# A fused retention layer and two MLPs: four mixed steps issued as 24 products, two outputs, two scores

## The chip, the cores and the metric

The kernel runs on one core of a Trainium2 chip. The core has five engines with a queue of instructions each: TensorE (PE) multiplies matrices, VectorE (DVE), ScalarE (ACT) and GpSimd (POOL) work on elements, SyncE (SP) starts the DMA transfers here. An engine takes its instructions in the order in which the program issues them; engines wait for each other by semaphores. The metric is the time of one execution on the device in microseconds (us); lower is better.

## The reference

A retention layer (linear attention with a decay per head) gives x, and two MLPs follow it. In float32, cut to the core:

```python
for t in range(S):                                   # B=2, H=8, S=768, D=64
    state = gamma * state + outer(k[t], v[t])
    y[t] = (1 / sqrt(D)) * q[t] @ state
x = y as (1536 tokens, 512)
h = x @ w_in;  g = softplus(h);            x = g @ w_out      # 512 -> 2048 -> 512
h = x @ w_in2; g = s * relu(h) ** 2 + b;   return g @ w_out2
```

## The kernel before

**Retention.** The 768 positions of a batch are cut into 6 chunks of 128; with 2 batches there are 12 chunks, and each is worked on in two units of four heads, so there are 24 units. A unit has *scores* (`att_scores`, L150: 8 small matmuls k by q into PSUM, then the decay mask on DVE writes tile `a`) and *outputs* (`att_out`, L173: `st` by `q2`, `a` by v, and the update of the state into the right half of the same PSUM bank). What follows a unit's outputs is in `unit` (L430): ACT copies the output to `xh` (`x_hi`), DVE adds the update to the decayed state (`sm`), ACT writes it to `st` in two pieces and decays the state of the unit before (`sg`, two pieces), and DVE writes the rest `xl` (`x_lo`). POOL scales q and v of the next chunk.

**MLPs.** A float32 operand is split into a high part (`xh`, `wh`, `gh`) and a low part (`xl`, `wl`, `gl`), and a product of two is three matmuls: 12 for a step's h (`h_mm`) and 12 for its share of the output sums (`acc_mm`). A step is a block of 128 hidden units by a tile of 512 tokens. `act_0` to `act_3` make g from h, `act_hi` (ACT) and `act_lo` (POOL or DVE) split it. `acc_mm` of a step is issued three steps later in the first part of the program, and two later after that. Four steps make a group; then `take_out` (L370) copies the four sums out of PSUM.

**Weights.** A float64 weight half comes by DMA and is put together and split by `split_w` (L259): three DVE instructions write the word `wx` (before step 3 a lent PSUM bank, `acc`), ACT squares (`wm<-raw`), a fourth DVE instruction writes `wm`, ACT copies it to `wh`, POOL subtracts to get `wl`. `fill(n)` issues the next n of these four DVE stages; the last stage brings `wh` and `wl` with it.

**Order.** It is written out by hand (`manual_schedule`). First eight units run alone (L506). Steps 0 to 2 (`early`, L519) have h products and two units each, with two units' score banks in turn: `un`, and two lent accumulation banks, whose mask is two DVE instructions (L168). Steps 3 to 7 (`mixed`, L536) have in turn: 12 h products, a unit's outputs, scores of a later unit, 12 sum products, the second unit's outputs, scores. The step's weight half is finished (`fill(2)`) at its very end, after both units and both masks. The half that `mixed` or its successor finishes in step 3, 4 or 5 is the one that `acc_mm` of the next step uses: halves (1,1), (2,1) and (3,1), the second number 1 being the half for the sums. In step 6 the sums of steps 0 to 3 are copied out on ACT, and step 7 begins new sums in their banks. From step 8 on (L567) there are only products: 40 steps of 24.

Of the kernel before, what the change touches and what calls it, by code (L numbers as in the profile page):

```python
# [7 lines left out]
F32 = mybir.dt.float32  # L8
# [3 lines left out]
ALU = mybir.AluOpType  # L12

P = 128
# [4 lines left out]
C = 128  # L19
# [26 lines left out]
def tile_retention_mlps(ctx: ExitStack, tc: tile.TileContext, qk, kv, w1, w2, sb, consts, out):  # L46
# [8 lines left out]
    wp = ctx.enter_context(tc.tile_pool(name="w", bufs=RING))  # L55
    gp = ctx.enter_context(tc.tile_pool(name="g", bufs=LAG_U + 1))
    tp = ctx.enter_context(tc.tile_pool(name="t", bufs=2))
    ps_acc = ctx.enter_context(tc.tile_pool(name="ps_acc", bufs=4, space=bass.MemoryType.PSUM))
    ps_h = ctx.enter_context(tc.tile_pool(name="ps_h", bufs=1, space=bass.MemoryType.PSUM))
    ps_y = ctx.enter_context(tc.tile_pool(name="ps_y", bufs=1, space=bass.MemoryType.PSUM))  # L60
    ps_s = ctx.enter_context(tc.tile_pool(name="ps_s", bufs=1, space=bass.MemoryType.PSUM))

    def bank(pool, tag):
        return pool.tile([P, 512], F32, tag=tag, name=tag)

    cst = cp.tile([P, CW], F32, tag="cst", name="cst")
    vtab = cst[:, 0:H]
# [18 lines left out]
        return scored[0] == NU and not a_t  # L86


    ac = [bank(ps_acc, "acc") for _ in range(KC)]

    def word():
        if fill.at >= LAG_U:
# [46 lines left out]
    def scale_q(ci):  # L139
# [7 lines left out]
        )  # L147
        q2_t[ci] = t

    def att_scores(n, banks):  # L150

        ci, f = divmod(n, HF)
        t = qk_t[ci]

        def of(h):
            return banks[h] if isinstance(banks, tuple) else banks[:, h, :HC]

        for i in range(HP):
            p = f * HP + i
            for h in range(2):  # L160
                r = slice(h * D, (h + 1) * D)
                nc.tensor.matmul(  # L162
                    of(h)[:, i * C : (i + 1) * C], t[r, 1, p], t[r, 0, p], start=True, stop=True
                )
        a = ap_.tile([P, 2, HC], F32, tag="a", name="a")
        if isinstance(banks, tuple):
            for h in range(2):
                nc.vector.tensor_tensor(out=a[:, h], in0=banks[h], in1=mask[:, f, h], op=ALU.mult)  # L168
        else:
            nc.vector.tensor_tensor(out=a, in0=banks[:, :, :HC], in1=mask[:, f], op=ALU.mult)  # L170
        a_t[n] = a

    def att_out(n, y):  # L173
# [119 lines left out]
    steps = [(la, g, j, f4) for la in range(2) for g in range(NG) for j in range(NTILE) for f4 in range(FG)]  # L293
    h_t, l_t, gg_t, acc_t = {}, {}, {}, {}

    def h_mm(s, part):
        la, g, j, f4 = steps[s]
        wh, wl = w_t[la * NF + g * FG + f4, 0]
        if part == 0:
            h_t[s] = bank(ps_h, "h") if s < SB or s % 2 else bank(ps_y, "y")  # L300
        ps = h_t[s]
        for cc in (0, 1) if part == 0 else (2, 3):
            wa, wb = (w[:, cc * P : (cc + 1) * P] for w in (wh, wl))
            for i, (l, r) in enumerate(((wa, xh), (wa, xl), (wb, xh))):
                nc.tensor.matmul(  # L305
                    ps, l, r[j][:, cc, :], start=cc == 0 and i == 0, stop=cc == KC - 1 and i == 2
                )
# [14 lines left out]
    def act_1(s):  # L322
        if steps[s][0] == 0:

            nc.scalar.activation(l_t[s], l_t[s], AF.Softplus)  # L325
# [24 lines left out]
    def act_lo(s, eng=None):  # L350
        gh, gl = gg_t[s]
        (eng or nc.vector).tensor_tensor(out=gl, in0=l_t.pop(s), in1=gh.bitcast(F32), op=ALU.subtract)  # L352

    def acc_mm(s, banks):
        la, g, j, f4 = steps[s]
        wh, wl = w_t[la * NF + g * FG + f4, 1]
        gh, gl = gg_t[s]
        if (la, g, j) not in acc_t:
            acc_t[la, g, j] = [bank(ps_acc, "acc") for _ in range(KC)] if acc_t else ac
        for cc in banks:  # L360
            cs = slice(cc * P, (cc + 1) * P)
            ps = acc_t[la, g, j][cc]
            if la == 0:
                ops = ((wh[:, cs], gh), (wh[:, cs], gl), (wl[:, cs], gh))
            else:
                ops = ((gh[:, cs], wh), (gh[:, cs], wl), (gl[:, cs], wh))
            for i, (l, r) in enumerate(ops):
                nc.tensor.matmul(ps, l, r, start=f4 == 0 and i == 0, stop=f4 == FG - 1 and i == 2)  # L368
# [76 lines left out]
                load_next()  # L445
            load_kv(ci + NIN)

    def score_to(n, banks):
        while scored[0] < min(n, NU):
            att_scores(scored[0], banks(scored[0]))  # L450
            scored[0] += 1

    def own(n):
        return un

    def lent(n):

        return un if n % HF == 0 else (ac[0][:, :HC], ac[1][:, :HC])

    def out_of(y):  # L460
        return y[:, :HC], y[:, HC : HC + HP * D]
# [15 lines left out]
    with tc.manual_schedule():  # L477
        fill.at = -1
        nc.scalar.preload_act_table_set("softplus")
        nc.vector.memset(zero, 0.0)  # L480
        nc.vector.memset(st, 0.0)
        nc.vector.memset(cu[:, 0:1], 0xC0000000)
        nc.vector.memset(cu[:, 1:2], 29)
        load_qk(0)
        nc.sync.dma_start(out=cst[:, :CG], in_=consts[:, :CG])
        load_kv(0)
        nc.sync.dma_start(out=cst[:, CG:], in_=consts[:, CG:])
        load_qk(1)
        load_kv(1)
        load_qk(2)  # L490
        load_next()
        load_kv(2)
        load_qk(3)
        load_kv(3)

        def warm(bank, key):
            for _ in range(WARM[key]):
                nc.tensor.matmul(bank[:, 0:P], zero[:, 0:P], zero[:, P : 2 * P], start=True, stop=True)

        ys = [bank(ps_h, "h"), bank(ps_y, "y")]  # L500
        warm(ac[3], "first")
        scale_q(0)
        scale_v(0)
        score_to(2, lent)
        warm(ac[3], "u0")
        for n in range(N0):  # L506
            if n >= len(ys):
                ys.append(bank(*((ps_h, "h"), (ps_y, "y"))[n % 2]))
            unit(n, out_of(ys[n]))
            if n == 1:  # L510
                load_next()
                load_next()
                nc.sync.dma_start(out=sbt, in_=sb)
                warm(ac[3], "s2")

            score_to((2, 4, 4, 6, 7, 8, 9, 10)[n], lent)
            fill((0, 0, 0, 2, 1, 1, 0, 4)[n])

        def early(s):  # L519

            fill.at = s
            n = N0 + HF * s
            h_mm(s, 0)
            h_mm(s, 1)
            act_0(s)
            unit(n, out_of(bank(ps_y, "y")), lambda: act_1(s))
            score_to(n + 3, lent)
            act_2(s)
            act_3(s)
            unit(n + 1, out_of(ac[3]))  # L530
            act_hi(s)
            score_to(n + 4, lent)
            act_lo(s, nc.gpsimd)
            fill(4)

        def mixed(s):  # L536

            old = s - LAG_U
            fill.at = s
            n = N0 + HF * s  # L540
            h_mm(s, 0)
            h_mm(s, 1)
            act_0(s)
            unit(n, out_of(bank(ps_y, "y")), lambda: act_1(s))
            score_to(n + 3, own)
            act_2(s)
            act_3(s)
            act_hi(s)
            fill(2)
            acc_mm(old, FIRST)  # L550
            acc_mm(old, SECOND)
            unit(n + 1, out_of(bank(ps_y, "y")))
            score_to(n + 4, own)
            act_lo(s, nc.gpsimd)
            if steps[old][3] == FG - 1:
                for cc in range(KC):
                    take_out(old, cc)
            fill(2)

        for s in range(SB):  # L560
            (early if s < LAG_U else mixed)(s)
        for old in range(SB - LAG_U, SB - LAG):
            acc_mm(old, FIRST)
            acc_mm(old, SECOND)
        fill(left[0])
        work = iter(())
        for s in range(SB, NS + LAG):  # L567
            run, old, prev = s < NS, s - LAG, s <= NS
            takes = steps[old][3] == FG - 1
            late = work  # L570
            work = split_next(s + 1) if run and not takes else iter(())
            if run:
                h_mm(s, 0)
                h_mm(s, 1)
                act_0(s)
            if prev and s > SB:
                act_3(s - 1)
            go(work, 2)
            if run:
                acc_mm(old, FIRST)  # L580
                if takes:
                    take_out(old, 0)
                    take_out(old, 1)
                act_1(s)
            if prev and s > SB:
                act_hi(s - 1)
            if run:
                act_2(s)
            go(late, 1)
            if prev and s > SB:  # L590
                act_lo(s - 1)
            if run:
                acc_mm(old, SECOND)
                if takes:
                    take_out(old, 2)
                    take_out(old, 3)
            go(work, 2)

        for banks in (FIRST, SECOND[:1], SECOND[1:]):
            for old in (NS - 2, NS - 1):  # L600
                acc_mm(old, banks)
            for cc in banks:
                take_out(NS - 1, cc)
# [70 lines left out]
```

## Time and profile before

| | |
|---|---|
| time, median of 3 runs | 587.14 us (587.09 to 587.19) |
| profiled execution | 587.26 us, span 585.3 us |
| busy, share of the span | PE 98%, DVE 78%, ACT 38%, POOL 23% |
| PE clock granted | 9 tenths or more in all 40 slices |
| chain that ended last | PE 91%, DVE 4%, ACT 2% |

The span is the time from the first instruction to the last; 1.96 us of the profiled execution lie outside it. A busy engine counts from the start to the modelled end of its instructions, and matmuls overlap by about 0.16 us, so PE's own pace is read from the starts of its instructions. A row of a timeline has the start, the length, the engine, the line and operation, the tiles written and read, the shape, the count of merged instructions, and in brackets the idle time before it with what ended it.

### The profile page before, as it was taken

To read this page: it belongs to the slowest core of one execution; us is meant where nothing else is said; L and a number is where in the kernel's file an instruction comes from. 1 tells how busy PE (TensorE), PEld (TensorE's weight loads), DVE (VectorE), ACT (ScalarE), POOL (GpSimd) and SP (SyncE) were. 2 spreads that over 40 slices of the span, in tenths; PEclk is the share of its full clock that TensorE was granted. 3 is DMA by queue.
4 is the path that set the end of the run, shared out by engine and by line. 5 is a ranking of instruction groups with operands and counts; after the bars stand their busy time and mean duration, and the time that the engine had idled before them with its cause. 6 is when DMAs were issued, how large, how long until landed. Compare 5 with 4: busy or idle time off the path is not lost.

```text
span 585.3 us, 7917 instructions
## 1 busy us (share of the span) xinstructions
PE 574.0 (98%) x3028; PEld 472.8 (81%) x3028; DVE 454.2 (78%) x700; ACT 223.7 (38%) x441; POOL 137.4 (23%) x109
## 2 busy tenths in 40 slices
PE   7989999999999999999999999999999999999997
PEld 6767777888888888888888888888888888888885
DVE  3898665688899897899869997888877886984553
ACT  3656554454333333333434532333333332332121
POOL 3456532021121120021433420121101110110000
PEclk9999999999999999999999999999999999999999
DMA  8976212122222221222212221222112122000111
GB/s 327 415 289 205 79 38 72 64 81 73 68 76 72 73 72 37 72 73 72 69 41 73 71 73 44 65 72 88 57 38 94 50 72 67 5 1 0 73 72 73
DMA packets 14869, 50.58 MB, mean 86 GB/s; under 512 B 1776, under 2 KB 1776, under 8 KB 14832
## 3 DMA queue, kind: packets, MB, share of 16 engines
q1 hardware_dynamic: 14832, 50.08, 24.9%
q8 instruction: 24, 0.39, 0.3%
q14 instruction: 13, 0.11, 0.1%
HBM read 46.93 MB, written 3.15 MB: 86 GB/s over the span
## 4 chain that ended last, share of the span: by engine, by line
PE 91%; DVE 4%; ACT 2%; DMA 1%; issue 1%; POOL 0%; SPq 0%; DVEq 0%; POOLq 0%
PE acc L368 45%; PE h L305 22%; PE y L305 20%; PE y L182 2%; DMA kv<-kv 1%; PE s L162 1%; DVE a L168 1%; DVE xl L220 1%; DVE a L170 1%; ACT xh L214 1%; DVE acc L273 1%; ACT st L240 1%; DVE acc L278 1%; DVE wm L284 0%; ACT wh L101 0%
## 5 line engine op out<-in xcount | busy, mean ns | idle before, releaser
L104 POOL TENSOR_TENSOR wl<-wm,wh 128x512 fp32r<-128x512 f32 x64 | 86.4, 1350 | 360.6 <-ACT wh L101 325.4
L352 DVE TENSOR_TENSOR gl<-t,gh 128x512 fp32r<-128x512 f32 x88 | 84.9, 965 | 6.3 <-ACT gh L348 6.2
L305 PE MATMUL h<-xh,wh 128*128 128x512 f32 x208 | 81.8, 394 | 2.8 <-DVE t L330 2.6
L305 PE MATMUL h<-xl,wh 128*128 128x512 f32 x208 | 81.1, 390 | 0.0
L305 PE MATMUL h<-xh,wl 128*128 128x512 f32 x208 | 81.0, 389 | 0.0
L368 PE MATMUL acc<-gh,wl 128*128 128x512 f32 x192 | 74.9, 390 | 0.6 <-POOL wl L104 0.6
L368 PE MATMUL acc<-gh,wh 128*128 128x512 f32 x192 | 75.4, 393 | 0.0
L368 PE MATMUL acc<-gl,wh 128*128 128x512 f32 x192 | 74.9, 390 | 0.0
L368 PE MATMUL acc<-wh,gh 128*128 128x512 f32 x192 | 74.7, 389 | 0.0
L368 PE MATMUL acc<-wl,gh 128*128 128x512 f32 x192 | 74.7, 389 | 0.0
L368 PE MATMUL acc<-wh,gl 128*128 128x512 f32 x192 | 74.7, 389 | 0.0
L325 ACT ACTIVATE t<-t 128x512 f32<-128x512 f32 x48 | 30.2, 629 | 102.0 <-DVE t L314 102.0
L305 PE MATMUL y<-xh,wh 128*128 128x512 f32 x176 | 68.5, 389 | 0.0
L305 PE MATMUL y<-xl,wh 128*128 128x512 f32 x176 | 68.5, 389 | 0.0
L305 PE MATMUL y<-xh,wl 128*128 128x512 f32 x176 | 68.5, 389 | 0.0
L378 DVE TENSOR_TENSOR xa<-acc,xa 128x512 f32<-128x512 f32 x72 | 47.2, 683 | 20.1 <-PE acc L368 20.1
L348 ACT ACTIVATE gh<-t 128x512 fp32r<-128x512 f32 x96 | 59.6, 621 | 3.9 <-DVE t L330 2.5
L330 DVE SCALAR_TENSOR_TENSOR t<-h,t 128x512 f32<-128x512 f32 x52 | 35.6, 685 | 23.5 <-ACT t L319 16.1
L305 PEld LDWEIGHTS h<-xh,wh 128*128 128x128 f32 x208 | 38.9, 187 | 11.8 <-DVE t L330 3.2
L319 ACT ACTIVATE t<-h 128x512 f32<-128x512 f32 x24 | 14.4, 599 | 88.4 <-PE h L305 88.4
L319 ACT ACTIVATE t<-y 128x512 f32<-128x512 f32 x24 | 14.4, 598 | 85.0 <-PE y L305 85.0
L276 ACT ACTIVATE wm<-raw 128x512 f32<-128x512 f32 x64 | 42.2, 659 | 9.8 <-POOL wl L104 9.8
(84 smaller groups left out, 952.1 us busy)
## 6 DMA issues: line engine op xcount, KB each, us to landing
raw<-w SPq DMA_DIRECT2D x64, 512.0 KB, 3.7
qk<-qk SPq DMA_DIRECT2D x12, 512.0 KB, 7.8
kv<-kv SPq DMA_DIRECT2D x12, 512.0 KB, 8.3
out<-xa SPq DMA_DIRECT2D x12, 256.0 KB, 2.0
cst<-consts SPq DMA_DIRECT2D x1, 518.0 KB, 4.2
cst<-consts SPq DMA_DIRECT2D x1, 256.0 KB, 6.4
sbt<-sb SPq DMA_DIRECT2D x1, 1.0 KB, 9.0
```

The costliest lines, as they stand in the source:

```text
L104: lo_eng.tensor_tensor(out=lo, in0=src, in1=hi.bitcast(F32), op=ALU.subtract)
L162: nc.tensor.matmul(of(h)[:, i * C : (i + 1) * C], t[r, 1, p], t[r, 0, p], start=True, stop=True)
L182: nc.tensor.matmul(y[to][h * D : (h + 1) * D, cols], l, r, start=h not in done, stop=True, skip_group_check=True)
L276: nc.scalar.activation(m, hw.bitcast(F32), AF.Square)
L305: nc.tensor.matmul(ps, l, r[j][:, cc, :], start=cc == 0 and i == 0, stop=cc == KC - 1 and i == 2)
L319: nc.scalar.activation(t1, ps, AF.Relu)
L325: nc.scalar.activation(l_t[s], l_t[s], AF.Softplus)
L330: nc.vector.scalar_tensor_tensor(out=t2, in0=ps, scalar=0.0, in1=l_t[s], op0=ALU.max, op1=ALU.add if steps[s][0] == 0 else ALU.mult,)
L348: nc.scalar.activation(gg_t[s][0], l_t[s], AF.Copy)
L352: (eng or nc.vector).tensor_tensor(out=gl, in0=l_t.pop(s), in1=gh.bitcast(F32), op=ALU.subtract)
L368: nc.tensor.matmul(ps, l, r, start=f4 == 0 and i == 0, stop=f4 == FG - 1 and i == 2)
L378: nc.vector.tensor_tensor(out=dst, in0=ps, in1=dst, op=ALU.add)
```

## The change

Steps 4 to 7 are issued by a new function, `grouped`: 12 h products, 12 sum products, the outputs of both units, the scores of two later units. The outputs of the first unit go to whichever of the two banks `h` and `y` the step's h is not in, those of the second to the bank of the step's own h, and h of the steps from 4 on alternates between the two. Both scores lie side by side in the two banks of `un`. Masks are issued after all scores of a call, and in `grouped` the end of the weight half (`fill(2)`) ahead of them. In `early` that `fill` comes ahead of the POOL half of `act_lo`. The first two accumulation banks become one tile, `acc01`, so that a mask on lent banks is one instruction.

```diff
-    ps_acc = ctx.enter_context(tc.tile_pool(name="ps_acc", bufs=4, ...))
+    ps_acc = ctx.enter_context(tc.tile_pool(name="ps_acc", bufs=1, ...))
+    def sums():
+        t = ps_acc.tile([P, 2, 512], F32, tag="acc01", name="acc01")
+        return [t[:, 0], t[:, 1], bank(ps_acc, "acc2"), bank(ps_acc, "acc3")], t
...
-    ac = [bank(ps_acc, "acc") for _ in range(KC)]
+    ac, ac01 = sums()
...
+    masks = []
...
-        if isinstance(banks, tuple):
-            for h in range(2):
-                nc.vector.tensor_tensor(out=a[:, h], in0=banks[h], in1=mask[:, f, h], op=ALU.mult)
-        else:
-            nc.vector.tensor_tensor(out=a, in0=banks[:, :, :HC], in1=mask[:, f], op=ALU.mult)
+        masks.append(
+            lambda: nc.vector.tensor_tensor(out=a, in0=banks, in1=mask[:, f], op=ALU.mult)
+        )
...
+    def two_banks(i):
+        return bank(ps_y, "y") if i % 2 else bank(ps_h, "h")
...
-            h_t[s] = bank(ps_h, "h") if s < SB or s % 2 else bank(ps_y, "y")
+            h_t[s] = two_banks(s if s > LAG_U else 0)
...
-    def score_to(n, banks):
+    def score_to(n, banks, work=lambda: None):
+
         while scored[0] < min(n, NU):
             att_scores(scored[0], banks(scored[0]))
             scored[0] += 1
+        work()
+        while masks:
+            masks.pop(0)()
 
     def own(n):
-        return un
+        f = n % HF
+        return un[:, :, f * HC : (f + 1) * HC]
 
     def lent(n):
-        return un if n % HF == 0 else (ac[0][:, :HC], ac[1][:, :HC])
+        return (ac01 if n % HF else un)[:, :, :HC]
...
             score_to(n + 4, lent)
+            fill(4)
             act_lo(s, nc.gpsimd)
-            fill(4)
...
+        def grouped(s):
+
+            old = s - LAG_U
+            fill.at = s
+            n = N0 + HF * s
+            h_mm(s, 0)
+            h_mm(s, 1)
+            act_0(s)
+            act_1(s)
+            act_2(s)
+            act_3(s)
+            act_hi(s)
+            fill(2)
+            acc_mm(old, FIRST)
+            acc_mm(old, SECOND)
+            unit(n, out_of(two_banks(s + 1)))
+            unit(n + 1, out_of(two_banks(s)))
+            score_to(n + 2 * HF, own, lambda: fill(2))
+            act_lo(s, nc.gpsimd)
+            if steps[old][3] == FG - 1:
+                for cc in range(KC):
+                    take_out(old, cc)
+
         for s in range(SB):
-            (early if s < LAG_U else mixed)(s)
+            (early if s < LAG_U else mixed if s == LAG_U else grouped)(s)
```

On PE in step 4 of the kernel before, from the last h product over both units to the first product of step 5 (`y`, `acc`, `s` are PSUM tiles, `q`, `a`, `v` what a unit's outputs read):

```order
L305 MATMUL h<-xh_101,wl_287 128x512
L182 MATMUL y<-q_716,st 64x128 x4
L182 MATMUL y<-a,kv 64x128 x4
L182 MATMUL y<-v_718,kv 64x64 x4
L162 MATMUL s<-qk 128x128 x4
L368 MATMUL acc<-gh,wh_731 128x512
...
L368 MATMUL acc<-gh,wl_732 128x512
L182 MATMUL y<-q_716,st 64x128 x4
...
L162 MATMUL s<-qk 128x128 x4
L305 MATMUL h<-xh_101,wh_420 128x512
```

The same place in the changed kernel:

```order
L310 MATMUL h<-xh_101,wl_283 128x512
L373 MATMUL acc_109<-gh,wh_722 128x512
L373 MATMUL acc_109<-gl,wh_722 128x512
L373 MATMUL acc_109<-gh,wl_723 128x512
...
L184 MATMUL y<-q_707,st 64x128 x4
L184 MATMUL y<-a,kv 64x128 x4
L184 MATMUL y<-v_709,kv 64x64 x4
L184 MATMUL h<-q_707,st 64x128 x4
L184 MATMUL h<-a,kv 64x128 x4
L184 MATMUL h<-v_709,kv 64x64 x4
L166 MATMUL s<-qk 128x128 x8
L310 MATMUL y<-xh_101,wh_414 128x512
```

The first unit's outputs and the first scores have moved from between the two product groups to behind them, and the third sum product, the first to read `wl`, now follows 14 products after the step's beginning.

On DVE in step 4, after the act_2 of that step, first before and then changed (`wx` and `wm` are the weight half, `sm` and `xl` follow a unit's outputs, `a` is a mask):

```order
L269 TENSOR_SCALAR wx_840<-raw_517 128x512
L273 SCALAR_TENSOR_TENSOR wx_840<-raw_517,cu_96,wx_840 128x512
L237 TENSOR_TENSOR sm_98<-sg_99,y_857 128x128
L220 TENSOR_TENSOR xl2_105<-y_857,xh2_102 128x2x128
L170 TENSOR_TENSOR a_881<-s_113,cst_94 128x512
L278 SCALAR_TENSOR_TENSOR wx_840<-raw_517,cu_96,wx_840 128x512
L284 SCALAR_TENSOR_TENSOR wm_841<-wm_841,wx_840 128x512
```

In the changed kernel:

```order
L271 TENSOR_SCALAR wx_801<-raw_509 128x512
L275 SCALAR_TENSOR_TENSOR wx_801<-raw_509,cu_96,wx_801 128x512
L239 TENSOR_TENSOR sm_98<-sg_99,y_818 128x128
L222 TENSOR_TENSOR xl2_105<-y_818,xh2_102 128x2x128
L239 TENSOR_TENSOR sm_98<-sg_99,h_842 128x128
L222 TENSOR_TENSOR xl2_105<-h_842,xh2_102 128x2x128
L280 SCALAR_TENSOR_TENSOR wx_801<-raw_509,cu_96,wx_801 128x512
L286 SCALAR_TENSOR_TENSOR wm_802<-wm_802,wx_801 128x512
L171 TENSOR_TENSOR a_866<-s_112,cst_94 128x512
L171 TENSOR_TENSOR a_871<-s_112,cst_94 128x512
```

The last two stages of the weight half stand ahead of the masks now, and behind `sm` and `xl` of both units instead of the second unit alone, as before.

On ACT in step 6 of the changed kernel, from the weight's square over both units to the copies of the sums (`xa`):

```order
L278 ACTIVATE wm_1008<-raw_665 128x512
L216 ACTIVATE xh2_102<-y_1024 128x2x128
L242 ACTIVATE st_97<-sm_98 64x2x64 x2
L249 ACTIVATE sg_99<-sm_98,cst_94 128x64 x2
L216 ACTIVATE xh2_102<-h_1046 128x2x128
L242 ACTIVATE st_97<-sm_98 64x2x64 x2
L106 ACTIVATE wh0_1005<-wm_1008 128x512
L379 ACTIVATE xa0_106<-acc01_109 128x512 x2
L379 ACTIVATE xa0_106<-acc2_110 128x512
L379 ACTIVATE xa0_106<-acc3_111 128x512
```

The second unit's `xh` stands behind `st` and `sg` of the first with nothing of the products' work between them any more, and `wh` ahead of the four copies; before, the copies stood ahead of it.

## Rows read from the trace of the kernel before

**Rows 1.** Busy time by stretch: us, PE, PEld, DVE, ACT, POOL, clock, DMA share, GB/s.

```profile
56.70:66.40 9.70, 9.70 (x91) 7.75 (x89) 6.37 (x13) 5.42 (x14) 5.26 (x4) 1.00 0.35 110
93.80:580.00 486.20, 486.16 (x2145) 402.27 (x2144) 387.22 (x565) 171.00 (x306) 90.81 (x68) 1.00 0.18 60
```

**Rows 2.** Timeline of PE: start, length, instruction, in brackets idle time and releaser.

```profile
52.26 0.50 PE L368 MATMUL acc<-gh,wl 128*128 128x512 f32 x1 [0.61 <-POOL wl L104]
...
54.78 0.66 PE L182 MATMUL y<-q,st 128*64 128x128 f32 x8
...
56.68 0.50 PE L305 MATMUL h<-xh,wh 128*128 128x512 f32 x1
...
62.10 0.40 PE L368 MATMUL acc<-gh,wl 128*128 128x512 f32 x1
...
66.40 0.50 PE L305 MATMUL h<-xh,wh 128*128 128x512 f32 x1
...
85.86 0.50 PE L305 MATMUL h<-xh,wh 128*128 128x512 f32 x1
...
88.83 0.66 PE L182 MATMUL y<-q,st 128*64 128x128 f32 x8
...
93.82 0.50 PE L368 MATMUL acc<-gh,wh 128*128 128x512 f32 x1
...
99.39 0.39 PE L368 MATMUL acc<-gh,wh 128*128 128x512 f32 x1
```

**Rows 3.** Timelines of ACT, DVE, POOL: end of weight half (1,1).

```profile
56.15 0.38 ACT L214 ACTIVATE xh<-y 128x256 fp32r<-128x256 f32 x1 [1.95 <-PE y L182]
...
57.70 0.74 DVE L278 SCALAR_TENSOR_TENSOR wx<-raw,cu,wx 128x512 uint32<-128x512 uint32 x1
...
58.55 0.69 DVE L284 SCALAR_TENSOR_TENSOR wm<-wm,wx 128x512 f32<-128x512 f32 x1
...
59.28 0.63 ACT L101 ACTIVATE wh<-wm 128x512 fp32r<-128x512 f32 x1 [1.13 <-DVE wm L284]
...
59.98 1.27 POOL L104 TENSOR_TENSOR wl<-wm,wh 128x512 fp32r<-128x512 f32 x1 [3.66 <-ACT wh L101]
```

**Rows 4.** Timeline of all engines: two units back to back, chunk 1.

```profile
12.99 0.61 PE L182 MATMUL y<-q,st 128*64 128x128 f32 x8
...
13.20 0.38 ACT L214 ACTIVATE xh<-h 128x256 fp32r<-128x256 f32 x1 [0.63 <-PE h L182]
...
14.19 0.72 PE L162 MATMUL s<-qk 64*128 64x128 f32 x8
...
15.10 0.36 ACT L214 ACTIVATE xh<-y 128x256 fp32r<-128x256 f32 x1
...
15.29 0.66 PE L182 MATMUL h<-q,st 128*64 128x128 f32 x8
...
16.03 0.68 DVE L170 TENSOR_TENSOR a<-s,cst 128x512 f32<-128x512 f32 x1
```

**Rows 5.** Timeline of ACT: the four copies of sums in step 6.

```profile
86.72 2.07 ACT L374 ACTIVATE xa<-acc 128x512 f32<-128x512 f32 x4
```

**Rows 6.** Timeline of DVE: first and last of six two-piece masks.

```profile
16.63 0.75 DVE L168 TENSOR_TENSOR a<-acc,cst 128x256 f32<-128x256 f32 x2
...
17.30 0.68 DVE L269 TENSOR_SCALAR acc<-raw 128x512 uint32<-128x512 uint32 x1
...
46.47 0.74 DVE L168 TENSOR_TENSOR a<-acc,cst 128x256 f32<-128x256 f32 x2
```

**Rows 7.** Waits of all engines, 9 to 57 us: total, times, longest.

```profile
POOL wl L104 <- ACT wh L101: 13.3, 5, 3.6
```

**Rows 8.** Timelines of DVE and POOL beside each other, step 3.

```profile
53.78 1.41 DVE L273 SCALAR_TENSOR_TENSOR wx<-raw,cu,wx 128x512 uint32<-128x512 uint32 x1
...
53.42 1.23 POOL L136 TENSOR_TENSOR v<-kv,cst 128x512 f32<-128x512 f32 x1
...
54.61 1.72 POOL L352 TENSOR_TENSOR gl<-t,gh 128x512 fp32r<-128x512 f32 x1
```

**Rows 9.** Timeline of DVE: after a group's sums are taken, layer 0.

```profile
193.16 1.28 DVE L378 TENSOR_TENSOR xa<-acc,xa 128x512 f32<-128x512 f32 x2
...
195.55 1.28 DVE L378 TENSOR_TENSOR xa<-acc,xa 128x512 f32<-128x512 f32 x2
...
197.51 0.69 DVE L314 TENSOR_SCALAR t<-y 128x512 uint32<-128x512 uint32 x1 [0.68 <-PE y L305]
```

More of the change, by code (lines that the diff above doesn't have):

```diff
@@ L57, in tile_retention_mlps @@
     tp = ctx.enter_context(tc.tile_pool(name="t", bufs=2))
-    ps_acc = ctx.enter_context(tc.tile_pool(name="ps_acc", bufs=4, space=bass.MemoryType.PSUM))
+    ps_acc = ctx.enter_context(tc.tile_pool(name="ps_acc", bufs=1, space=bass.MemoryType.PSUM))
     ps_h = ctx.enter_context(tc.tile_pool(name="ps_h", bufs=1, space=bass.MemoryType.PSUM))
@@ L153, in att_scores @@
         t = qk_t[ci]
-        def of(h):
-            return banks[h] if isinstance(banks, tuple) else banks[:, h, :HC]
         for i in range(HP):
@@ L162, in att_scores @@
                 nc.tensor.matmul(
-                    of(h)[:, i * C : (i + 1) * C], t[r, 1, p], t[r, 0, p], start=True, stop=True
+                    banks[:, h, i * C : (i + 1) * C], t[r, 1, p], t[r, 0, p], start=True, stop=True
                 )
         a = ap_.tile([P, 2, HC], F32, tag="a", name="a")
-        if isinstance(banks, tuple):
-            for h in range(2):
-                nc.vector.tensor_tensor(out=a[:, h], in0=banks[h], in1=mask[:, f, h], op=ALU.mult)
-        else:
-            nc.vector.tensor_tensor(out=a, in0=banks[:, :, :HC], in1=mask[:, f], op=ALU.mult)
+        masks.append(
+            lambda: nc.vector.tensor_tensor(out=a, in0=banks, in1=mask[:, f], op=ALU.mult)
+        )
         a_t[n] = a
@@ L358, in acc_mm @@
         if (la, g, j) not in acc_t:
-            acc_t[la, g, j] = [bank(ps_acc, "acc") for _ in range(KC)] if acc_t else ac
+            acc_t[la, g, j] = sums()[0] if acc_t else ac
         for cc in banks:
```

## The prediction

> **What bounds the kernel now.** I read the page first, then busy time by stretch, then timelines of the stretch that the change touches. PE is the bound nearly everywhere: in the stretch from 93.80 us on it is busy for 486.16 of 486.20 us, and in step 4 (56.70 to 66.40) for all of 9.70 [rows 1]. So nothing but instructions on PE sets the pace there, and a change to steps 4 to 7 can win only what PE spends in them, from 56.68 to 93.82 us: 37.14 us [rows 2]. Steps 4, 5 and 6 take (85.86 - 56.68)/3 = 9.73 us each, step 7 takes 7.96. The one stall near them is PE's 0.61 us at 52.26, where the third sum product of step 3 waits for `wl`, made by POOL [rows 2].
>
> Next is the question of how nearly PE waits there in the later steps. The chain that makes the half (1,1) is in rows 3: ACT's copy `xh` of the last unit starts at 56.15, DVE's third stage of the half at 57.70, `wm` at 58.55, `wh` at 59.28, `wl` at 59.98, done 1.27 later, 61.25. Its reader, the third sum product of step 4, starts at 62.10 [rows 2]. The chain has 0.85 us to spare, because a unit's outputs and a set of scores stand between the h products and the sum products. The change takes just these out of the way.
>
> **The early part.** Before 52 us the chain that ends last runs mostly through DVE, and six masks of two pieces lie on it. A pair takes 17.30 - 16.63 = 0.67 us to the next instruction [rows 6], the one-piece mask before it 16.63 - 16.03 = 0.60 [rows 4, 6]. One piece for two saves 0.067, six times: -0.39 us. Below, nothing if each saving is eaten by another wait; above, two more pairs that lie off the chain, -0.5. I take -0.39, since the DVE instructions behind the pairs start without idle time.
>
> `fill` ahead of `act_lo` in `early` moves only POOL's work: `wl` ahead of `gl`. I cost it at nothing: POOL waited for `wh` before each of five `wl`, 13.3 us in all [rows 7], so `wl` gains nothing from standing ahead, and `gl`, some 3 us later, is first read a step or more after. If that cover goes, q and v of the next chunk come one `gl` later, at most 1.7 us [rows 8].
>
> **Steps 4 to 7 as PE alone would do them.** Twenty-four products in a row take 99.39 - 93.82 = 5.57 us, against 2 x 2.97 (88.83 - 85.86) in two groups [rows 2]. The second of two adjacent units takes 14.19 - 12.99 = 1.20 and two adjacent scores 15.29 - 14.19 = 1.10 [rows 4]. With 1.2 for the first unit and 0.1 for leaving the products, a step would be 9.17 instead of 9.73: -0.56, three times. Step 7, with two units in 7.96 - 5.94 = 2.02 and no scores, would be 7.69: -0.27. With the early part -2.3 us. This holds only if nothing is late.
>
> The Trainium skill has a rule for this gain (TensorEngine Tiling (Array Packing), Key Properties): a change of the tiling mode drains TensorE. Fewer changes between 64-row scores, outputs and products would then pay, and by the rule alone the time would come to the 584.8 us of the first rival below. The rows agree on the size of a change but say nothing of what PE then waits for.
>
> **What is late then: `wl` in steps 4, 5 and 6.** Step 4 first. Its half is finished in step 3, whose order stays, so the time from `xh` at 56.15 to `wl` at 61.25 and 0.05 for the release stays. The third sum product is now the fifteenth product: 14/24 of 5.57 and 0.05 after 56.68, 59.98. It waits till 61.30: a stall of 1.3 us. From such a restart to the next unit's outputs takes 54.78 - 52.26 = 2.52, and from there to that unit's `xh` 56.15 - 54.78 = 1.37 [rows 2, 3]. So `xh` of unit 16 starts at 61.30 + 2.52 + 1.37 = 65.19.
>
> Now a full period, from `xh` of one step's first unit to that of the next. The trace has two units back to back in chunk 1, with the same queue on ACT (`xh`, two `st`, two `sg`, `xh`) and on DVE: the first `xh` at 13.20, the second only at 15.10, though PE had left the second unit at 14.19, and DVE is through with both at 16.03, 2.83 after the first `xh` [rows 4]. The weight half's third stage stands next on DVE. From its start to the release of `wl` is 61.30 - 57.70 = 3.60 [rows 3]. Then 2.52 and 1.37 again: 2.83 + 3.60 + 2.52 + 1.37 = 10.32 us, against 9.73 before. That `fill` stands ahead of the two masks helps (behind them `wl` would be 1.2 later), but it stands behind both units' `sm` and `xl`. The masks have their cover: they are read after the next 24 products. So `xh` of unit 18 starts at 75.51, of unit 20 at 85.83. The stall in steps 5 and 6 is some 1.05: h products would begin 2.1 after `xh` (1.20 + 1.10 less the 0.21 from 12.99 to 13.20), the third sum product 3.3 later, at 5.4, and `wl` comes at 6.43.
>
> **Step 7.** Its sums go into banks that ACT must first empty, and the copies now stand behind both units and behind `wh`. `wh` starts 2.83 + 0.85 + 0.73 = 4.41 after `xh` of unit 20 and takes 0.63; two of the four copies take half of 2.07 [rows 5], and as the first two banks are one tile now, both must be done: 85.83 + 6.1 = 91.95. PE alone would be there at 2.1 + 2.85 = 4.95: a stall of 1.15. Then 2.97 for the sum products and 2.02 for the two units: step 7 ends at 96.95, not 93.82, +3.13. Less the early 0.39: +2.74 us.
>
> From step 8 on order and tiles are the same but for the shared tile: `take_out` of the first bank now waits for the products of both, 3 x 0.23 = 0.7 us later. DVE has 0.68 idle after a group's copies [rows 9], h has two banks so that DVE may be a step late, and PE never waited there [rows 1]: nothing.
>
> One more cost has no row of its own. `gl` of step 2 now runs after `wl`, and pushes q, v and `gl` of step 3 back on POOL by 1.3 us, to where DVE does the last stages of half (1,1). Beside POOL's v and `gl`, DVE's second stage took 1.41 [rows 8], the third alone 0.74 [rows 3]. Bounds: nothing, or +0.67 once; I take nothing, since POOL should be through by then to within a tenth or two. The Trainium skill (SBUF — State Buffer, SBUF: two separate sides) calls this a lock: a DVE instruction with two SBUF inputs and a GpSimd one block each other wholly. By that rule a DVE stage would wait out the rest of `gl`, a few tenths; the rows (1.41 and 1.72 side by side) agree in kind.
>
> **Sum.** The profiled execution, 587.26 us (1.96 outside the span), would be 590.0. The median of the runs lies 0.12 below it: 587.14 + 2.74 = 589.9 us. By stalls: -2.3 for PE alone, +1.3 +1.05 +1.05 +1.15, and a tenth for each restart, gives +2.6, near enough.
>
> **Rivals.** *`wl` is not late* (other side): PE is the bound of the grouped steps as of the old ones, and the time falls by 2.3 to 584.8. It decides at a chain from `xh` to `wl` of 5.4 us or less instead of 6.43. For it: PE is at its limit now, and the pieces of the change fit this aim. Against it: every link of the 6.43 is a measured start to start on queues whose order is known.
>
> *ACT is not in the way*: the second `xh` starts when its unit is done, 1.1 after the first instead of 1.90. Then `wl` and the copies come 0.8 sooner, two periods are 9.52 and step 7 is 0.8 shorter: 2.74 - 2.4 = +0.3, 587.5 us, no change. Against it stands the second `xh` at 15.10 [rows 4].
>
> *The shared tile costs in every group*: the 0.7 us is not absorbed in 24 groups. If 0.3 of each reached PE, 7 us more, 597. Against it: rows 1 and 9.
>
> **How the numbers follow.** The forecast has 0.82, the first rival 0.08, the second 0.06, the third 0.04. A difference under 0.2% (1.17 us) can't be told from none. The forecast lies wholly on the slow side, its own range 588.6 to 591.0: the early gain from 0 to 0.5, each of the four stalls within 0.2, POOL's +0.67. So faster 0.08, same 0.06, slower 0.86. The range of 8 in 10 is 588.0 to 591.2, wider below because a shorter chain shortens three stalls at once, and above for the POOL cost on top of longer stalls.
>
> **What would show it.** In the new profile PE should wait for `wl` in the third sum product of steps 4, 5 and 6, 1.0 to 1.3 us each, and in step 7 for ACT's copies, some 1.1; the second `xh` of a step should start 1.9 after the first; steps 5 and 6 should be 10.3 us long; masks before step 3 one piece of 0.60; from step 8 on PE should not wait. I am wrong if steps 4 to 6 are near 9.2 without a wait of PE, or if PE waits after step 8.

## The result and the profile after

The changed kernel takes 590.79 us, the median of 4 runs (589.78 to 591.25), against 587.16 before (4 runs, 587.09 to 587.54): a ratio of 1.0059 [1.0047, 1.0071]. It is slower by 3.6 us, where 2.7 were forecast (589.9). The profiled execution takes 591.25 us with a span of 588.3, 3.0 more than the span before. In the four runs the span is 587.4, 588.3, 588.0 and 588.4.

The timeline of PE in the changed kernel, steps 4 to 7; the columns are those of [rows 2]:

```profile
56.48 0.50 PE L310 MATMUL h<-xh,wh 128*128 128x512 f32 x1
...
59.70 0.50 PE L373 MATMUL acc<-gh,wh 128*128 128x512 f32 x1 [0.18 <-ACT wh L106]
...
61.05 0.50 PE L373 MATMUL acc<-gh,wl 128*128 128x512 f32 x1 [0.62 <-POOL wl L109]
...
63.54 0.66 PE L184 MATMUL y<-q,st 128*64 128x128 f32 x8
...
66.99 0.50 PE L310 MATMUL y<-xh,wh 128*128 128x512 f32 x1
...
71.28 0.50 PE L373 MATMUL acc<-gh,wl 128*128 128x512 f32 x1 [0.62 <-POOL wl L109]
...
77.24 0.50 PE L310 MATMUL h<-xh,wh 128*128 128x512 f32 x1
...
81.60 0.51 PE L373 MATMUL acc<-gh,wl 128*128 128x512 f32 x1 [0.62 <-POOL wl L109]
...
87.58 0.50 PE L310 MATMUL y<-xh,wh 128*128 128x512 f32 x1
...
91.48 0.50 PE L373 MATMUL acc<-gh,wh 128*128 128x512 f32 x1 [0.89 <-ACT xa L379]
...
94.43 0.66 PE L184 MATMUL h<-q,st 128*64 128x128 f32 x8
...
96.33 0.50 PE L373 MATMUL acc<-gh,wh 128*128 128x512 f32 x1
```

Steps 4, 5 and 6 begin at 56.48, 66.99, 77.24 and end at 87.58: 10.51, 10.25 and 10.34 us, against 9.73 before. In each the third sum product, the first to read `wl`, waits for POOL. In step 7 the first sum product waits for the copies on ACT. From the first h product of step 4 to the first product after step 7 are 96.33 - 56.48 = 39.85 us; before, 37.14 [rows 2]. The bracket counts idle time only from the modelled end of the product before: from 59.70 to 61.05 are 1.35 us for two products. Back to back two take 2/24 of 5.57 [rows 2], 0.46, and about 0.1 more after a stop; the other 0.8 are lost to the wait for `wl`. The first sum product is late too, for `wh`: by 0.34 us in step 4 (the 0.18 in the bracket at 59.70), by 0.06 and 0.12 in steps 5 and 6, where no bracket shows it, counted from the starts of it and of the last h product.

The chain to `wl` of step 5, from the timelines of ACT, DVE and POOL, which answers [rows 3, 4]:

```profile
64.91 0.38 ACT L216 ACTIVATE xh<-y 128x256 fp32r<-128x256 f32 x1 [1.98 <-PE y L184]
...
66.81 0.36 ACT L216 ACTIVATE xh<-h 128x256 fp32r<-128x256 f32 x1
...
67.74 0.74 DVE L280 SCALAR_TENSOR_TENSOR wx<-raw,cu,wx 128x512 uint32<-128x512 uint32 x1
...
69.24 0.63 ACT L106 ACTIVATE wh<-wm 128x512 fp32r<-128x512 f32 x1 [0.47 <-DVE wm L286]
...
69.95 1.28 POOL L109 TENSOR_TENSOR wl<-wm,wh 128x512 fp32r<-128x512 f32 x1 [6.53 <-ACT wh L106]
...
75.16 0.38 ACT L216 ACTIVATE xh<-h 128x256 fp32r<-128x256 f32 x1 [1.47 <-PE h L184]
```

From the first unit's `xh` (64.91) to the second's (66.81) are 1.90 us, to the weight half's third stage 2.83, both to the hundredth as in chunk 1 [rows 4]; to `wl` 5.04 (5.11 forecast: 2.83, and 2.28 from the third stage to `wl` in [rows 3]); to the next `xh` of a first unit 10.25.

The copies of step 6, ACT's timeline, which answers [rows 5]:

```profile
85.50 0.38 ACT L216 ACTIVATE xh<-y 128x256 fp32r<-128x256 f32 x1 [1.50 <-PE y L184]
...
89.83 0.63 ACT L106 ACTIVATE wh<-wm 128x512 fp32r<-128x512 f32 x1 [1.08 <-DVE wm L286]
...
90.37 2.04 ACT L379 ACTIVATE xa<-acc 128x512 f32<-128x512 f32 x4
```

From unit 20's `xh` at 85.50, `wh` begins 4.33 later (4.41 forecast) and the four copies stand behind it; PE goes on at 91.48, 5.98 after that `xh` (91.95 - 85.83 = 6.12 forecast).

The first of the one-piece masks on lent banks, DVE's timeline, which answers [rows 6]: 0.60 us to the next instruction.

```profile
16.85 0.68 DVE L171 TENSOR_TENSOR a<-acc,cst 128x512 f32<-128x512 f32 x1
...
17.45 0.68 DVE L271 TENSOR_SCALAR acc<-raw 128x512 uint32<-128x512 uint32 x1
```

Where the 3.0 us of span are: the transfers at the start land a little later in this execution, seen in DVE's first `sm`, here

```profile
9.80 0.29 DVE L237 COPY sm<-h 128x128 f32<-128x128 f32 x1 [2.68 <-ACT xh L216]
```

and before

```profile
9.59 0.29 DVE L235 COPY sm<-h 128x128 f32<-128x128 f32 x1 [2.74 <-ACT xh L214]
```

so 0.21 us come from the launch. It differs from execution to execution: e2_tile_alone, the same code up to there, has this `sm` at 9.43. From that `sm` to step 4 the time falls from 56.68 - 9.59 = 47.09 to 56.48 - 9.80 = 46.68: -0.41 (-0.39 forecast). Steps 4 to 7: +2.71. From step 8 to the last product: +0.84 (580.97 - 93.82 before, 584.32 - 96.33 after), forecast as nothing. The end behind the last product: -0.35, for which no run gives a cause. Sum: 0.21 - 0.41 + 2.71 + 0.84 - 0.35 = 3.0. The other 0.6 of the 3.6 lie outside the span, where no row shows anything: the profiled time less its span is 2.95, in the other three runs 2.38, 2.77 and 2.41, against 1.96 before. It goes with the grouped steps: its median is 2.02 us in the runs of the kernel before that ran beside the experiments, 2.03 in e2_tile_alone, which has the old order, and 2.3 to 2.6 in every kernel that has the grouped steps. What it is stays open.

The 0.84 us lie in two places. At the first of them, timelines of DVE, ACT and PE in the changed kernel:

```profile
282.98 1.29 DVE L383 TENSOR_TENSOR xa<-acc,xa 128x512 f32<-128x512 f32 x2 [0.19 <-PE acc L373]
...
283.70 1.29 ACT L106 ACTIVATE xh<-xa 128x512 fp32r<-128x512 f32 x2 [4.88 <-DVE xa L383]
...
284.90 0.61 ACT L330 ACTIVATE t<-t 128x512 f32<-128x512 f32 x1
...
285.54 0.69 DVE L335 SCALAR_TENSOR_TENSOR t<-y,t 128x512 f32<-128x512 f32 x1 [1.28 <-ACT t L330]
...
286.15 1.35 DVE L357 TENSOR_TENSOR gl<-t,gh 128x512 fp32r<-128x512 f32 x1
...
286.86 0.39 PE L373 MATMUL acc<-gh,wh 128*128 128x512 f32 x1
...
287.56 0.50 PE L373 MATMUL acc<-gl,wh 128*128 128x512 f32 x1 [0.32 <-DVE gl L357]
```

In the kernel before, DVE and PE at the same place:

```profile
280.20 1.28 DVE L378 TENSOR_TENSOR xa<-acc,xa 128x512 f32<-128x512 f32 x2
...
284.35 0.39 PE L368 MATMUL acc<-gh,wh 128*128 128x512 f32 x1
...
284.78 0.50 PE L368 MATMUL acc<-gl,wh 128*128 128x512 f32 x1
```

This is the last group of a token tile in layer 0, where ACT makes the next layer's `xh` from the copies. DVE's two copies wait 0.19 us for PE, because the first of them waits for both banks of the shared tile; before, they waited for nothing. ACT's `xh` waits for them, the softplus `t` stands behind `xh` on ACT, act_2 on DVE waits for it (285.54, [1.28]), `gl` comes behind that, and PE waits for `gl`: 287.56 - 286.86 = 0.70 between two products that are 0.23 apart otherwise, 0.47 too late. The second place, at 309.93, is alike. Before, the same chain was late too, but by 0.20 (284.78 - 284.35 = 0.43) and once. So 2 x 0.47 - 0.20 = 0.74 us are waits, and one more restart adds 0.1.

### The profile page after: what moved, and what is told of

Same layout as the page of the kernel before. It is cut to its first block, busy times and chain, and to the rows that moved or that the text cites. A ratio compares the mean times of both kernels' runs of the same rounds, so it can differ in the third digit from the quotient of the medians.

```text
span 588.3 us, 7899 instructions
## 1 busy us (share of the span) xinstructions
PE 575.0 (98%) x3028; PEld 473.0 (80%) x3028; DVE 455.0 (77%) x692; ACT 223.7 (38%) x441; POOL 134.4 (23%) x109
## 4 chain that ended last, share of the span: by engine, by line
PE 86%; DVE 4%; issue 3%; ACT 3%; POOL 2%; DMA 1%; SPq 0%; POOLq 0%; DVEq 0%
PE acc L373 43%; PE h L310 20%; PE y L310 20%; DMA kv<-kv 1%; DVE a L171 1%; PE h L184 1%; PE y L184 1%; POOL q L150 1%; POOL gl L357 1%; POOL v L141 1%; ACT xh L216 1%; ACT st L242 1%; POOL wl L109 0%; DVE xl L222 0%; DVE wm L286 0%
## 5 line engine op out<-in xcount | busy, mean ns | idle before, releaser
L109 POOL TENSOR_TENSOR wl<-wm,wh 128x512 fp32r<-128x512 f32 x64 | 83.9, 1312 | 371.3 <-ACT wh L106 340.5
L310 PE MATMUL h<-xh,wh 128*128 128x512 f32 x200 | 78.5, 393 | 2.4 <-DVE t L335 2.4
L310 PE MATMUL h<-xl,wh 128*128 128x512 f32 x200 | 78.0, 390 | 0.0
L310 PE MATMUL h<-xh,wl 128*128 128x512 f32 x200 | 77.9, 389 | 0.0
L310 PE MATMUL y<-xh,wh 128*128 128x512 f32 x184 | 71.8, 390 | 0.0
L310 PE MATMUL y<-xh,wl 128*128 128x512 f32 x184 | 71.6, 389 | 0.0
L310 PE MATMUL y<-xl,wh 128*128 128x512 f32 x184 | 71.6, 389 | 0.0
L335 DVE SCALAR_TENSOR_TENSOR t<-y,t 128x512 f32<-128x512 f32 x46 | 31.5, 685 | 24.7 <-ACT t L324 14.6
L310 PEld LDWEIGHTS h<-xh,wh 128*128 128x128 f32 x200 | 37.5, 187 | 10.9 <-DVE t L335 3.0
```

Of the source, the lines that this page charges most:

```text
L109: lo_eng.tensor_tensor(out=lo, in0=src, in1=hi.bitcast(F32), op=ALU.subtract)
L310: nc.tensor.matmul(ps, l, r[j][:, cc, :], start=cc == 0 and i == 0, stop=cc == KC - 1 and i == 2)
L335: nc.vector.scalar_tensor_tensor(out=t2, in0=ps, scalar=0.0, in1=l_t[s], op0=ALU.max, op1=ALU.add if steps[s][0] == 0 else ALU.mult,)
```

## The experiments

Each kernel ran in 4 to 11 executions beside the kernel before (587.09 in the first four, 587.13 in the last four). The theory: PE waits in steps 4 to 7 for work that ACT and DVE put behind two units in a row, and after step 8 for the shared tile.

**e1_half_sooner**, the changed kernel with the weight half's stages moved:

```diff
-            fill(2)                                           # grouped
+            fill(3)
             acc_mm(old, FIRST)
             acc_mm(old, SECOND)
             unit(n, out_of(two_banks(s + 1)))
+            fill(1)
             unit(n + 1, out_of(two_banks(s)))
-            score_to(n + 2 * HF, own, lambda: fill(2))
+            score_to(n + 2 * HF, own)
...
-            fill(2)                                           # mixed, step 3
+            fill(3)
...
-            score_to(n + 4, own)
+            score_to(n + 4, own, lambda: fill(1))
...
-            fill(2)
```

> The weight half's third stage is issued with the first two, and its last stage between the two units (in step 3 ahead of the mask). If the late wl and the copies behind it are what steps 4 to 7 lost (theory), PE waits for wl no more in steps 4 to 6, steps 5 and 6 take 9.2 us, step 7 loses at most a few tenths to the copies, and the kernel takes 587.1 - 2.3 + 0.9 (the waits for gl after step 8 stay) = 585.7 us, 5 less than the changed one. If the grouped order itself costs and wl is only where the wait shows (rival), other waits take its place and it stays above 589.

Measured: 585.97 us (585.78 to 586.50), ratio to before 0.9985 [0.9976, 0.9994]. All waits of PE from step 4 on to 98 us, then the first h product of steps 4, 5 and 6 in its timeline:

```profile
PE acc L373 <- POOL wl L109: 0.2, 1, 0.2
...
56.01 0.50 PE L310 MATMUL h<-xh,wh 128*128 128x512 f32 x1
...
65.62 0.50 PE L310 MATMUL y<-xh,wh 128*128 128x512 f32 x1
...
74.76 0.50 PE L310 MATMUL h<-xh,wh 128*128 128x512 f32 x1
```

Of the four stalls 0.2 us of idle time in step 4 is left; by the starts the step takes 65.62 - 56.01 = 9.61 us. Step 5 takes 74.76 - 65.62 = 9.14 us, the 9.17 of PE alone: the order that PE got is worth what the prediction's first rival said, once `wl` is there. That rival had the size right and the condition wrong.

**e2_tile_alone**, the changed kernel with the old order of steps 4 to 7:

```diff
-            h_t[s] = two_banks(s if s > LAG_U else 0)
+            h_t[s] = bank(ps_h, "h") if s < SB or s % 2 else bank(ps_y, "y")
...
-            (early if s < LAG_U else mixed if s == LAG_U else grouped)(s)
+            (early if s < LAG_U else mixed)(s)
```

> The shared tile of the first two accumulation banks, the one-piece masks and the exchanged fill alone; steps 4 to 7 in the old order. If the shared tile makes the two new waits for gl after step 8 (theory), they are here too (two, 0.5 us of PE each, where the kernel before has one of 0.3) and the time is 587.1 - 0.4 + 0.9 = 587.6. If they come from the grouped steps (rival), they are gone and the time is 586.8.

Measured: 587.45 us (586.81 to 587.84), ratio 1.0007 [0.9998, 1.0016]. The two waits are there without the grouped steps, in PE's timeline:

```profile
284.51 0.50 PE L373 MATMUL acc<-gl,wh 128*128 128x512 f32 x1 [0.33 <-DVE gl L357]
...
306.89 0.50 PE L373 MATMUL acc<-gl,wh 128*128 128x512 f32 x1 [0.33 <-DVE gl L357]
```

**e3_own_tiles**, the changed kernel with `sums` giving four banks of their own, and masks on lent banks in two pieces again:

```diff
-        t = ps_acc.tile([P, 2, 512], F32, tag="acc01", name="acc01")
-        return [t[:, 0], t[:, 1], bank(ps_acc, "acc2"), bank(ps_acc, "acc3")], t
+        return [bank(ps_acc, f"acc{i}") for i in range(KC)], None
```

> The changed kernel with the two accumulation banks as tiles of their own and masks on them in two pieces. Theory (the shared tile makes the waits for gl): they are as before the change, one of 0.3, and the early 0.4 is lost: 590.8 - 0.9 + 0.4 = 590.3. Rival (they come from the grouped steps): they stay and the time rises by the early 0.4 to 591.2.

Measured: 589.70 us (589.03 to 589.95), 1.0045 [1.0031, 1.0058], 0.6 less than the theory's number. PE has no idle time after 98 us in the profile's count (by the starts the 0.2 us of the kernel before is there again, from 285.88 to 286.30), so the two longer waits for `gl` are the shared tile's, and the rival's 591.2 is out. From DVE's first `sm` (8.85) to step 4 (55.94) are 47.09 us again, as before the change, so the early 0.41 is the one-piece masks', and the exchanged `fill` has no part in it. The 0.6 has a part that I had not counted: step 7 no longer waits for two copies but for one. In PE's timeline the wait is 0.40, not 0.89:

```profile
90.50 0.50 PE L378 MATMUL acc<-gh,wh 128*128 128x512 f32 x1 [0.40 <-ACT xa L384]
```

**e4_both**, e1's and e3's edits together.

> Both: the half's stages sooner, and the banks as tiles of their own. Theory: 585.7 - 0.9 + 0.4 = 585.2, with no wait of PE for wl in steps 4 to 6 and at most one for gl after step 8. Rival (the grouped order itself costs): above 588.

Measured: 585.73 us (584.61 to 585.89), 0.9974 [0.9964, 0.9984]. No wait for `gl` after step 8; it is 0.5 slower than expected. Between DVE's first `sm` and PE's last product it does what was expected: 579.48 - 9.74 = 569.74 us, against 579.62 - 9.32 = 570.30 in e1_half_sooner, 0.56 less for 0.5. The profiled execution loses this gain ahead of that stretch, where `sm` comes 0.42 later, and behind the last product, where the span goes on 0.3 us longer (4.32, not 3.98). Why these two differ stays open.

**e5_pair_last**, e1 with the shared tile's banks last of the four:

```diff
-FIRST, SECOND = (0, 1), (2, 3)
+FIRST, SECOND = (2, 3), (0, 1)
...
-                for cc in range(KC):
+                for cc in FIRST + SECOND:
                     take_out(old, cc)
...
-                    take_out(old, 0)
-                    take_out(old, 1)
+                    for cc in FIRST:
+                        take_out(old, cc)
...
-        for banks in (FIRST, SECOND[:1], SECOND[1:]):
+        for banks in ((0, 1), (2,), (3,)):
```

> As e1_half_sooner, and the two banks of the shared tile are summed and copied last of the four (banks 2, 3, then 0, 1; the last group of all stays in the old order). If the waits for gl after step 8 come from the first copy's wait for the second bank of the shared tile (theory), they go: by the time DVE comes to the copies of a tile that ends last, both banks are done. 586.0 - 0.9 = 585.1, no wait of PE after step 8 or one of 0.3. If something else in that stretch makes gl late (rival): 586.0.

Measured: 585.13 us (584.42 to 585.29), 0.9965 [0.9953, 0.9978]; no idle time of PE after 98 us in the profile's count. One piece for the masks and no late copies can be had together.

**e6_masks_last**, e5 with the weight half ahead of the last mask in `early`:

```diff
-            score_to(n + 4, lent)
-            fill(4)
+            score_to(n + 4, lent, lambda: fill(4))
```

> As e5_pair_last, and in steps 0 to 2 the weight half is finished ahead of the last mask too. DVE sat idle 0.37 us after act_0 in each of steps 0 to 2 for xh, which stands behind wh on ACT; with wm 0.6 sooner that goes, three times, and the wait for wl in step 3 (0.6 and 0.1 to restart) goes as well: 585.1 - 1.1 - 0.6 = 583.4. If the masks are then late for the units of the next step (rival), PE waits for a mask in steps 1 to 3 and the gain is nothing or a loss.

Measured: 583.55 us (583.12 to 583.83), 0.9941 [0.9928, 0.9955], the fastest of all and faster than both kernels. The third sum product of step 3 waits for nothing now (its row in PE's timeline), and in step 1 DVE puts the mask between `wm` and act_0 of that step (its timeline):

```profile
49.68 0.50 PE L373 MATMUL acc<-gh,wl 128*128 128x512 f32 x1
...
34.39 0.69 DVE L286 SCALAR_TENSOR_TENSOR wm<-wm,acc 128x512 f32<-128x512 f32 x1
...
34.99 0.69 DVE L171 TENSOR_TENSOR a<-acc,cst 128x512 f32<-128x512 f32 x1
...
35.59 0.68 DVE L319 TENSOR_SCALAR t<-h 128x512 uint32<-128x512 uint32 x1
```

No mask was late. The idle 0.37 us went in steps 1 and 2 alone, not in step 0, whose `fill` was not moved.

**e7_decay_ahead**, the changed kernel with `sg` of both units issued behind the second, for the next step (`dec=False` keeps `unit` from issuing it):

```diff
+            if s == LAG_U + 1:
+                decay(n - 1)
...
-            unit(n, out_of(two_banks(s + 1)))
-            unit(n + 1, out_of(two_banks(s)))
+            unit(n, out_of(two_banks(s + 1)), dec=False)
+            unit(n + 1, out_of(two_banks(s)), dec=False)
+            decay(n)
+            decay(n + 1)
```

> The changed kernel with the decay (sg, two ACT instructions) taken out from between the two units' xh and issued after both, for the next step. If ACT's queue sets the second xh and with it wl and the copies (theory), xh comes 0.49 sooner, steps 5 and 6 take 9.8 instead of 10.3 us, the copies come 0.5 sooner: 590.8 - 1.5 = 589.3. If ACT is not in the way (rival, the second of the prediction): no change, 590.8.

Measured: 589.05 us (588.84 to 589.25), 1.0033 [1.0021, 1.0046]. ACT's timeline in step 4, then three starts of PE:

```profile
64.45 0.38 ACT L216 ACTIVATE xh<-y 128x256 fp32r<-128x256 f32 x1 [1.98 <-PE y L184]
...
65.84 0.38 ACT L216 ACTIVATE xh<-h 128x256 fp32r<-128x256 f32 x1
...
70.34 0.50 PE L373 MATMUL acc<-gh,wl 128*128 128x512 f32 x1 [0.32 <-POOL wl L109]
...
80.21 0.50 PE L373 MATMUL acc<-gh,wl 128*128 128x512 f32 x1 [0.43 <-POOL wl L109]
...
89.59 0.50 PE L373 MATMUL acc<-gh,wh 128*128 128x512 f32 x1 [0.40 <-ACT xa L379]
```

The second `xh` comes 1.39 us after the first instead of 1.90, and PE waits 0.32 and 0.43 for `wl` in steps 5 and 6, and 0.40 for the copies. So ACT's queue is a link of the chain, and the prediction's second rival is out.

**e8_masks_first**, the changed kernel with `fill(2)` behind the masks:

```diff
-        work()
         while masks:
             masks.pop(0)()
+        work()
```

> The changed kernel with the weight half's end behind the two masks in steps 4 to 7. Theory: wl and the copies come 1.2 us later, and PE waits that much longer in steps 5, 6 and 7: 590.8 + 3.6 = 594.4. If the masks don't stand in the chain (rival): no change.

Measured: 595.54 us (595.22 to 596.57), 1.0148 [1.0134, 1.0161], 1.1 more than expected. PE's timeline in steps 6 and 7 shows where:

```profile
81.98 0.50 PE L373 MATMUL acc<-gh,wh 128*128 128x512 f32 x1 [1.16 <-ACT wh L106]
...
83.33 0.50 PE L373 MATMUL acc<-gh,wl 128*128 128x512 f32 x1 [0.62 <-POOL wl L109]
...
87.08 0.97 PE L184 MATMUL y<-q,st 128*64 128x128 f32 x8
...
95.94 0.50 PE L373 MATMUL acc<-gh,wh 128*128 128x512 f32 x1 [2.05 <-ACT xa L379]
```

The waits are as expected: 1.16 more in step 6, for `wh`, ahead of the same 0.62 for `wl`, and in step 7 2.05 for the copies, not 0.89. But ten products behind the waits of step 6 take 87.08 - 83.33 = 3.75 us, against 2.52 [rows 2]: from 84.4 on they are 0.43 apart, not 0.23. In busy time by stretch the granted clock (the figure before the last two) is half there:

```profile
84.40:87.10 2.70, 2.70 (x9) 1.68 (x7) 0.96 (x1) 0.15 (x1) 2.10 (x2) 0.50 0.00 0
```

## Why the prediction was right

The chain of steps 4 to 6 was right link by link: `xh` to `xh` 1.90, to the third stage 2.83, the period 10.25 and 10.34 for 10.32. e1, e7 and e8 moved links of it, and the time followed, by 4.8, 1.7 and 4.8 us (some 1.5 of the last by the clock). Step 4 came out 0.1 shorter than worked out (`xh` 8.43 us after its start, not 8.51) and step 7 by 0.3 (10.83 from unit 20's `xh` to its end, not 11.12): the copies were 0.14 sooner, and the two last units took 96.33 - 94.43 = 1.90, not 2.02. So steps 4 to 7 are at +2.71 for +3.13, the early part at -0.41 for -0.39. The waits themselves were named too long: the third sum product loses 0.8 us to `wl` in steps 4 to 6, not 1.0 to 1.3. The prediction let PE run on to that product, and PE stops for `wh` at the first one already and then restarts once more. The period is the same either way, since the chain through `wl` sets it.

The step that failed is the one on the shared tile, "nothing": PE does wait after step 8, which the prediction had named as a sign of being wrong. The delay of the first copy and the idle 0.68 on DVE [rows 9] were right, but I looked at a group where nothing else hangs on the copies. In the last groups of layer 0 ACT's `xh` hangs on them, and act_2 on that: 0.3 us of delay reached PE in two of 24 groups, +0.84 in all (24 groups are 96 steps, so 88 steps follow step 7, not the 40 of the description above). This was the third rival's mechanism, at an eighth of its 7 us. That the forecast of the total came as near as 0.9 us is in part luck: steps 4 to 7 cost 0.42 less than forecast and the shared tile 0.84 more, which cancel in part, and 0.6 us outside the span is left unexplained.

POOL's term was rightly nothing: POOL's `gl` is through at 56.13 + 1.28 = 57.41, just ahead of the third stage of half (1,1), which takes 0.74 as before (first two rows). DVE's second stage did stretch beside POOL's q, as [rows 8] showed it beside v and `gl` (timelines of DVE and POOL, steps 3 and 5):

```profile
57.51 0.74 DVE L280 SCALAR_TENSOR_TENSOR wx<-raw,cu,wx 128x512 uint32<-128x512 uint32 x1
...
56.13 1.28 POOL L357 TENSOR_TENSOR gl<-t,gh 128x512 fp32r<-128x512 f32 x1
...
72.83 1.66 DVE L275 SCALAR_TENSOR_TENSOR wx<-raw,cu,wx 128x512 uint32<-128x512 uint32 x1
...
72.43 1.51 POOL L150 TENSOR_TENSOR q<-qk,cst 128x512 f32<-128x512 f32 x1
```

This agrees in kind with the lock of which the Trainium skill speaks (SBUF — State Buffer, SBUF: two separate sides): 1.66 us for the second stage, where the third, of the same shape and clear of POOL, takes 0.74. The third stage, which stands on the chain, keeps its 0.74 in step 4's half too (67.74 above).

## What to carry to other kernels

Before work is taken out from between two stages of the bound engine, look for what was made in its shadow: here the weight half had 0.85 us to spare, and removing 1.9 us of other work ahead of its reader turned a bound engine into a waiting one. The period that follows can be read off the trace beforehand where the same queue order occurs elsewhere, as in chunk 1 here. In this kernel a tile that joins two banks joined their waits: let such a tile be the last that is written and read, as in e5, and follow each reader to what it feeds on every engine, in each kind of group.

## What the runs showed of the hardware

In e8_masks_first TensorE's granted clock fell to the lower of its two levels (0.50, 1.2 instead of 2.4 GHz) from 84.4 us until shortly after 87.1 (0.64 from 87.1 to 88.0, 1.00 from 88.0 on), while PE was busy again, about 1 us after two waits of 1.16 and 0.62. It cost 1.2 us on ten products and 0.3 on the units and scores behind them. In the changed kernel, with waits of 0.62 alone in steps 5 and 6, the clock stayed at 1.00 in these steps. So a stall cost time again behind its end. Which stalls do so these runs don't show: two waits of 1.09 and 0.62 in step 5 of the same run, and the 2.05 in step 7, had no such stretch behind them (1.00 from 66 to 82 and from 93 to 110 us).
